# Sliding-window attention with a gated conv FFN: attention output turned by DMA for batches 2 to 7, and a re-planned lead-in

## The chip, the cores and the metric

One core of a Trainium2 chip runs the whole program. In the views PE is the tensor engine (its weight loads are PEld), DVE is VectorE, ACT is ScalarE, POOL is GpSimd, and SPq is the sync queue, which issues DMA transfers. PEclk is the granted clock of PE, as a share of full speed. The metric is device time in microseconds (us). Most of the numbers below come from the profile of one execution ("span") or from a few timed runs.

## The reference, cut to what matters

```python
# q, k, v: [8 batches, 8 heads, 576 positions, 64]
scores = where(|i - j| <= 32, q @ k.T / 8, -1e9)
x = softmax(scores) @ v          # -> [8, 576, 512] (heads side by side)
h = relu(x @ w_in)               # 512 -> 1024
conv = sum_k conv_w[k] * shift(h, k - 1)      # 3 taps along the sequence
out = (h * sigmoid(conv)) @ w_out             # 1024 -> 512, float32
```

The first FFN product contracts over the 512 features, so each batch's attention output (positions on the partitions, features along the row) has to be turned: features onto partitions. That turn is the subject.

## The kernel before

The work is cut into jobs. Each job has a planned time and a list of jobs that must precede it, and jobs are given out in the order of the planned times. Planned times set an order, and which jobs of the lead-in (the stage before the first output) are held in program order; nothing else. Inside one kernel a scheduler still moves instructions unless they are marked `fixed`. The FFN runs in chunks of 384 positions, three for each pair of batches: `ph` (first product), `pc` (conv and gate), `py` (second product and a store).

The turn (`job_xt`): four 128x128 matmuls against the identity, then one PSUM copy on VectorE.

```python
def job_xt(b, c):                       # batch b, block c of 5
    ...
    ps = slot_f().rearrange("p (k x) -> p k x", k=KC)
    for kc in range(KC):
        nc.tensor.matmul(ps[:, kc, 0:cols], xn[b][:, c, 2 * kc:2 * kc + 2, :]..., ident[:, 0:cols], ...)
    (vector.tensor_copy if b > 1 or c % 2 else nc.scalar.copy)(
        out=xT[b // 2][:, :, b % 2, 128 * c:128 * c + cols], in_=ps[:, :, 0:cols])
```

The value tile is needed twice, once shifted by 64 partitions (`vo`). For batch 1 VectorE copies it, for later batches a DMA from the ScalarE queue:

```python
def shift_v(b):
    for p0, src in ((0, ve[64:128, 0:NBLK - 1]), (64, ve[0:64, 1:NBLK])):
        if b == 1:
            vector.tensor_copy(out=vo[p0:p0 + 64], in_=src)
        else:
            fixed(nc.scalar.dma_start(vo[p0:p0 + 64], src))
```

Planned times that matter here (`P` = 29 us per batch, `NP` = 4 head pairs per batch):

```python
T0, T1 = 22.0, 42.5                     # start of chunk 0, second half of chunk 1
...                                     # start[c]: later chunks
end = start[3 * (b // 2) + 1] - 3.0 - (0 if b % 2 else 20.0 if b == 2 else P)
d = P / NP if b > 3 else 5.0            # spacing of the four head pairs of batch b
s0 = max(end - 5.9 * d, pair[b * NP - 1][0] + d)      # first head pair
...
at(("xt", b, c), t + (2.0 + 0.06 * c) * d ...)        # turns, after the last head pair at t
```

Weights are loaded as float32 and cast to bf16 on GpSimd, half a weight (128x2048) to an instruction. During the lead-in only VectorE is held in program order (`vector.on`).

The softmax here doesn't subtract the row's maximum and nothing guards it: scores larger than these inputs give would overflow.

Of the kernel before, what the change touches and what calls it, by code (L numbers as in the profile page):

```python
# [17 lines left out]
def kernel(  # L18
# [58 lines left out]
    class InOrder:  # L77


        on = False  # L80

        def __getattr__(self, name):
            def give(*args, **kwargs):
                ins = getattr(nc.vector, name)(*args, **kwargs)  # L84
                return fixed(ins) if self.on else ins

            return give

    vector = InOrder()

# [41 lines left out]
    def shift_v(b):  # L132

        ve, vo = ve_pp[b % NLD], vo_pp[b % NLD]
        for p0, src in ((0, ve[64:128, 0:NBLK - 1]), (64, ve[0:64, 1:NBLK])):
            if b == 1:
                vector.tensor_copy(out=vo[p0:p0 + 64], in_=src)
            else:
                fixed(nc.scalar.dma_start(vo[p0:p0 + 64], src))

# [42 lines left out]
    def load_weight(src, dst, rows, cast_):  # L183

        n = src.shape[1] // 2
        for x in (0, n):
            st = {}

            def load(x=x, st=st):
                t_ = fpool.tile([128, rows * n], FP32, name="wst", tag="wst")  # L190
                st[0] = t_.rearrange("p (c f) -> p c f", c=rows)
                fixed(nc.sync.dma_start(
                    st[0], src.rearrange("(c p) f -> p c f", p=128)[:, :, x:x + n]
                ))

            yield load, lambda x=x, st=st: cast_(dst[:, :, x:x + n], st[0])

# [10 lines left out]
    def job_tr(g2, y):  # L208

        b, i = g2 // NPH, g2 % NPH  # L210
        nat = qkb_pp[b % NLD][y][i]
        to = []
        for g in (2 * g2, 2 * g2 + 1):
            if y == 0:
                t_ = apool.tile([128, S], BF16, name="qT", tag="qT", bufs=4)
                to.append(t_)
            else:
                t_ = kT_pp[g % NKT]
                to.append(t_[:, PAD:PAD + S])
            state["qk"[y], g] = t_  # L220

        small = b == 0
        for js in ((range(0, 4), range(4, 8), range(8, RP)) if small else (range(RP),)):
            j0, n = js[0], len(js)
            ps = slot_f() if small else slot_a()
            for j in js:
                nc.tensor.matmul(  # L227
                    ps[:, 128 * (j - j0):128 * (j - j0) + 128],
                    nat[:, j, :, :].rearrange("p e d -> p (e d)"),
                    ident, start=True, stop=True,  # L230
                )
            rows = ps[:, 0:128 * n].rearrange("p (j y x) -> p y x j", j=n, y=2)
            for x, copy in enumerate((nc.scalar.copy, vector.tensor_copy)):
                copy(
                    out=to[x].rearrange("p (x j) -> p x j", j=RP)[:, :, j0:j0 + n], in_=rows[:, x]
                )

    def job_conv_w():
        ps = slot_f()
        nc.tensor.matmul(ps[:, 0:3 * MB], conv_w24, ident24, start=True, stop=True)  # L240
        vector.tensor_copy(out=conv_w_sb.rearrange("p k m -> p (k m)"), in_=ps[:, 0:3 * MB])
# [8 lines left out]
    def job_sc(g):  # L250
        qT, kT = state.pop(("q", g)), state.pop(("k", g))
        ps, last = slot_a(), slot_f()
        for i in range(NT):
            for e, t in ((0, (i + NT - 1) % NT), (1, i)):
                nc.tensor.matmul(  # L255
                    last[:, 0:64] if e * t == NT - 1 else ps[:, col(e, t):col(e, t) + 64],
                    kT[64 * e:64 * e + 64, 64 * t:64 * t + 128],
                    qT[64 * e:64 * e + 64, 64 * t:64 * t + 64],
                    start=True, stop=True,
                )  # L260
        attn = apool.tile([128, 2 * S], BF16, name="attn", tag="attn", bufs=4)
        state["a", g] = attn
        x = 2 * S - 64
        nc.scalar.activation(attn[:, 0:x], ps[:, 0:x], AF.Exp, bias=0.0, scale=scale)  # L264
        nc.scalar.activation(attn[:, x:], last[:, 0:64], AF.Exp, bias=0.0, scale=scale)  # L265
        vector.tensor_tensor(out=attn, in0=attn, in1=mask, op=ALU.mult)

    def job_av(g):
# [7 lines left out]
        for e in range(2):  # L276
            for c in range(NBLK):
                for j in range(2):
                    t = min(2 * c + j, NT - 1)
                    nc.tensor.matmul(  # L280
                        pss[e][64 * j:64 * j + 64, 65 * c:65 * c + 65],
# [10 lines left out]
        for e, (po, rec, to) in enumerate(outs):  # L292
            if b == 0 and e == 1 and pr < 3:
                for c in range(NBLK):
                    nc.scalar.activation(
                        to[:, c, :], po[:, c, 0:64], AF.Copy, bias=0.0, scale=rec[:, c:c + 1]
                    )
# [6 lines left out]
    def job_xt(b, c):  # L304

        if b % 2 == 0 and c == 0:
            xT[b // 2] = fpool.tile([128, KC, 2, S], BF16, name="xT", tag="xT")
        cols = min(128, S - 128 * c)
        ps = slot_f().rearrange("p (k x) -> p k x", k=KC)
        for kc in range(KC):  # L310
            nc.tensor.matmul(  # L311
                ps[:, kc, 0:cols],
                xn[b][:, c, 2 * kc:2 * kc + 2, :].rearrange("p h d -> p (h d)"),
                ident[:, 0:cols], start=True, stop=True,
            )
        (vector.tensor_copy if b > 1 or c % 2 else nc.scalar.copy)(
            out=xT[b // 2][:, :, b % 2, 128 * c:128 * c + cols], in_=ps[:, :, 0:cols]
# [13 lines left out]
    def job_ph(c, m, halves=(0, 1)):  # L331
# [8 lines left out]
        for kc in range(KC):  # L340
            nc.tensor.matmul(  # L341
                ps[:, 0:n], w_in_sb[:, kc, m * 128:(m + 1) * 128], x_[:, kc, x0:x1],
                start=(kc == 0), stop=(kc == KC - 1),
            )
        if kind == 1:
            out_ = hT[:, m, :].rearrange("p (i x) -> p i x", i=2)
            for i in halves:
                o_ = out_[:, i, i:i + HW + 1]
                i_ = ps[:, (HW + 1) * (i - halves[0]):(HW + 1) * (i - halves[0]) + HW + 1]
                if halves == (0, 1):  # L350
                    continue
                nc.scalar.activation(o_, i_, AF.Relu, bias=0.0, scale=0.5)
            if halves == (0, 1):
                base = hT[:, m, 0:HW + 1]
                both = bass.AP(base.tensor, base.offset, [list(base.ap[0]), [HW + 3, 2], [1, HW + 1]])
                nc.scalar.activation(
                    both, ps[:, 0:n].rearrange("p (i x) -> p i x", i=2), AF.Relu, bias=0.0, scale=0.5
                )
        else:
            o0 = 1 if kind == 0 else 0  # L360
            nc.scalar.activation(hT[:, m, o0:o0 + n], ps[:, 0:n], AF.Relu, bias=0.0, scale=0.5)  # L361

    def job_pc(c, m, halves=(0, 1)):
# [14 lines left out]
        for kk in range(3):  # L378
            nc.tensor.matmul(  # L379
                ps[:, 0:n], diag_w[:, kk, m, :], taps(kk), start=(kk == 0), stop=(kk == 2)  # L380
            )
        tn = spool.tile([128, CH], FP32, name="tn", tag="tn")
        nc.scalar.activation(tn[:, 0:n], ps[:, 0:n], AF.Tanh, bias=0.0, scale=1.0)  # L383
        vector.scalar_tensor_tensor(
# [8 lines left out]
    def job_py(c, i):  # L393

        ps = slot_f()
        for m in range(MB):
            nc.tensor.matmul(  # L397
                ps, gT[c][:, m, 128 * i:128 * i + 128], w_out_sb[:, m, :],
                start=(m == 0), stop=(m == MB - 1),
            )  # L400
        y_sb = spool.tile([128, d_model], FP32, name="y_sb", tag="y_sb", bufs=4)
        nc.scalar.copy(out=y_sb, in_=ps)  # L402
        r0 = c * CH + 128 * i
# [16 lines left out]
    def give_out():  # L420
# [9 lines left out]
        while ready:  # L430
            _, _, key = heapq.heappop(ready)
            vector.on = plan[key][0] < T0 + 14.0
            plan[key][1]()
# [7 lines left out]

    T0, T1 = 22.0, 42.5
    start = {0: T0, 1: T1}
# [21 lines left out]
    for m in range(MB):  # L465
        at(("diag", m), T0 + 1.6 * m - 1.0, lambda m=m: make_diag(m), ("conv_w",))
    at(("conv_w",), 7.0, job_conv_w)
# [15 lines left out]
    for b in range(B):  # L483
# [4 lines left out]
        else:  # L488
            end = start[3 * (b // 2) + 1] - 3.0 - (0 if b % 2 else 20.0 if b == 2 else P)
            d = P / NP if b > 3 else 5.0  # L490
            s0 = max(end - 5.9 * d, pair[b * NP - 1][0] + d)
        for i in range(NP):
            pair[b * NP + i] = (s0 + i * d, d)
    for g in range(NG):
# [4 lines left out]
        if b == 0:  # L499
            t0, t1, t2, t3 = 5.8 + 1.35 * (g // 2) * 2, 7.2 + 1.35 * (g // 2) * 2, 8.4 + 2.0 * g, 16.2 + g  # L500
        else:
# [9 lines left out]
    for b in range(B):  # L511
        t, d = pair[b * NP + NP - 1]
        for c in range(NBLK):
            at(("xt", b, c), t + (2.0 + 0.06 * c) * d if b else 20.3 + 0.4 * c, lambda b=b, c=c: job_xt(b, c),
               *[("av", b * NP + i) for i in range(NP)],
               *[("ph", (b // 2 - 2) * 3 + 2, m, None) for m in range(MB)])
        t0 = pair[b * NP][0]
        for i, (ld, cs) in enumerate(load_stream(b)):
            if b == 0:
                x, y = -20.0, 20 + (4.3 + 1.35 * i if i < NP else 9.8 + 1.1 * (i - NP))  # L520
            elif b == 1:
# [3 lines left out]
            else:  # L525
                x, y = t0 - P - 3.0 + i * P / NV, 4.5
            at(("load", b, i), x, ld if b else lambda: None, ("load", b, i - 1),
               *[("cast", b - 1, j) for j in range(NV)],
# [8 lines left out]
    for i, (ld, cs) in enumerate(load_weight(moe_w_in, w_in_sb, KC, cast)):  # L537
        at(("w_in load", i), -1.0, ld, *[("load", 0, j) for j in range(NV)])
        at(("w_in", i), 16.5 + 2.0 * i, cs, ("w_in load", i))
    for i, (ld, cs) in enumerate(load_weight(moe_w_out, w_out_sb, MB, cast)):  # L540
# [33 lines left out]
```

## Time and profile before

| | us |
|---|---|
| time, median of 4 runs (of 3: 286.14) | 285.45 (284.67 to 286.53) |
| profiled span | 282.2 |
| PE busy | 246.8 (87%) |
| VectorE / ScalarE / GpSimd busy | 181.5 / 175.9 / 77.1 |

I cut each span at three events: the ScalarE copy of the first output rows of chunk 0, of the last rows of chunk 3, and of the first rows of chunk 9. That gives four stages: lead-in, first rounds (chunks 0 to 3 come out), later rounds (chunks 4 to 8), tail. This is the busy-time table of the kernel before for these stages. Its columns are the stretch, its length, the busy time of each engine with the number of instructions, the mean granted PE clock, the DMA share and GB/s.

```profile
core 0: us, PE busy (x) PEld busy (x) DVE busy (x) ACT busy (x) POOL busy (x), PEclk, DMA share, GB/s
0.00:71.34 71.34, 47.62 (x586) 33.88 (x588) 55.34 (x135) 39.37 (x93) 40.56 (x44) 0.90 0.87 251
71.34:143.53 72.19, 69.12 (x839) 42.85 (x847) 50.02 (x106) 49.70 (x105) 19.48 (x22) 1.00 0.62 170
143.53:249.22 105.69, 100.95 (x1079) 60.29 (x1094) 68.34 (x140) 68.73 (x139) 17.01 (x18) 1.00 0.43 123
249.22:282.20 32.98, 29.11 (x155) 15.19 (x156) 7.82 (x14) 18.14 (x36) 0.00 (x0) 0.99 0.20 72
```

In the lead-in PE is idle for 24 us and the mean clock is 0.90. The same table for those instructions alone that write or read the attention output `xn` shows what the turns cost PE in the two middle stages:

```profile
core 0: us, PE busy (x) PEld busy (x) DVE busy (x) ACT busy (x), PEclk, DMA share, GB/s
71.34:143.53 72.19, 3.18 (x40) 2.47 (x40) 10.13 (x22) 0.00 (x0) 1.00 0.62 170
143.53:249.22 105.69, 5.34 (x80) 4.91 (x80) 11.74 (x26) 0.00 (x0) 1.00 0.43 123
```

The PE columns are turns alone: 80 matmuls take 5.34 us of the later rounds, so a batch of 20 costs 1.33 us. The copies that follow them are in the view of the turned tile (duration in ns as minimum/median/maximum):

```profile
L84 DVE CAST xT<-pf x34: 406/680/693, 27.4 to 245.8; 128x512 bf16<-128x512 f32 x28, 128x256 bf16<-128x256 f32 x6
```

What PE waited for in the later rounds (total us, times, longest):

```profile
PE pf L379 <- DVE rec L84: 1.5, 2, 0.7
PE pa L227 <- DVE qT L84: 1.1, 2, 0.5
PE pf L341 <- DVE xT L84: 0.6, 1, 0.6
PE pf L255 <- DVE xT L84: 0.4, 1, 0.4
```

These named waits come to 3.6 us, all on VectorE, and only 1.0 us of that is on the copies of the turns (`xT`).

The bad place of the lead-in, in four-microsecond stretches:

```profile
36.00:40.00 4.00, 3.28 (x49) 1.73 (x47) 3.36 (x10) 3.46 (x8) 0.38 (x1) 1.00 1.08 358
40.00:44.00 4.00, 1.50 (x30) 1.21 (x29) 3.94 (x4) 1.47 (x2) 3.17 (x2) 0.80 1.06 390
44.00:48.00 4.00, 3.59 (x11) 1.30 (x10) 4.00 (x7) 1.46 (x4) 3.40 (x4) 0.50 1.17 273
48.00:52.00 4.00, 3.32 (x34) 2.31 (x35) 3.54 (x9) 1.06 (x3) 1.81 (x2) 0.50 0.40 89
```

VectorE is full from 40 to 48 us and PE waits. Then PE runs at half its clock until 52 us: it does 11 matmuls in a stretch in which it counts as 3.59 us busy. In that stretch a first-product matmul takes up to 0.53 us; the median of these over the span is 0.33 us. The Trainium skill ("TensorE: Matmul & The Clock Gate", Part 1) describes this: a clock gate at 4/8 after an idle window, 8/8 after sustained work.

### The profile page before, as it was taken

What the parts mean: (1) busy time and instruction counts of PE and PEld (TensorE: products, weight loads), DVE (VectorE), ACT (ScalarE), POOL (GpSimd) and SP (SyncE); (2) the same over time, 40 slices, a digit from 0 to 9 for tenths busy, and PEclk for the clock granted to TensorE, in tenths of its full rate; (3) what the DMA queues carried; (4) which work ended last, traced back from release to release, by engine and by line L of the source; (5) the groups of instructions that cost most, each with busy time, mean ns of one, the idle gap of its engine ahead of it and who ended that gap; (6) DMA issues with size and microseconds to landing.
All of it is one profiled execution on the core that took longest, in us unless ns stands there. A gap on an engine that the chain in (4) does not pass through costs nothing.

```text
span 282.2 us, 6681 instructions
## 1 busy us (share of the span) xinstructions
PE 246.8 (87%) x2652; PEld 152.2 (54%) x2682; DVE 181.5 (64%) x394; ACT 175.9 (62%) x370; POOL 77.1 (27%) x84
## 2 busy tenths in 40 slices
PE   1756767877999898999989999999989999999994
PEld 1535433656665554666555555565555655555551
DVE  5687989795465888486556767596656555733330
ACT  2755672565676666677765577766755677557652
POOL 5657738661026221043113412332200000000000
PEclk9999995797999999999999999999999999999999
DMA  6999999781687742784649564954240102011022
GB/s 231 253 329 360 210 365 256 193 280 32 171 207 239 199 114 66 231 272 118 148 95 310 156 161 131 306 165 114 65 115 37 39 37 78 37 39 74 37 78 112
DMA packets 55555, 45.58 MB, mean 162 GB/s; under 512 B 38860, under 2 KB 40932, under 8 KB 55524
## 3 DMA queue, kind: packets, MB, share of 16 engines
q1 hardware_dynamic: 54528, 41.95, 50.7%
q10 hardware_dynamic: 996, 3.21, 4.9%
q8 instruction: 21, 0.34, 0.6%
q14 instruction: 10, 0.08, 0.1%
HBM read 32.52 MB, written 9.44 MB: 149 GB/s over the span
## 4 chain that ended last, share of the span: by engine, by line
PE 70%; DVE 19%; ACT 5%; DMA 3%; issue 2%; SPq 1%; POOL 0%; DVEq 0%; ACTq 0%
PE pf L397 21%; PE pf L341 20%; PE pf L379 14%; PE pa L227 5%; PE pf L280 4%; DVE attn L84 3%; DVE xT L84 3%; DVE gT L84 3%; DMA kst<-in_k_dram 3%; DVE vo L84 3%; PE pa L255 3%; DVE diag_w L84 2%; ACT attn L264 2%; PE pf L311 2%; DVE xn L84 2%
## 5 line engine op out<-in xcount | busy, mean ns | idle before, releaser
L84 DVE SCALAR_TENSOR_TENSOR gT<-tn,hT 128x384 bf16<-128x384 f32 (+1 forms) x104 | 60.2, 587 | 43.2 <-ACT tn L383 42.9
L341 PE MATMUL pf<-xT,w_in_sb 128*128 128x385 bf16 (+2 forms) x416 | 81.3, 322 | 3.7 <-DVE xT L84 2.2
L379 PE MATMUL pf<-hT,diag_w 128*128 128x384 bf16 (+1 forms) x312 | 66.0, 320 | 2.6 <-DVE rec L84 1.5
L397 PE MATMUL pf<-w_out_sb,gT 128*128 128x512 bf16 x258 | 66.4, 380 | 1.6 <-issue 0.2
L383 ACT ACTIVATE tn<-pf 128x384 f32<-128x384 f32 (+1 forms) x104 | 49.0, 472 | 12.4 <-PE pf L379 11.8
L341 PEld LDWEIGHTS <-w_in_sb 128*128 128x128 bf16 x416 | 38.8, 100 | 27.1 <-DVE xT L84 2.0
L109 POOL TENSOR_SCALAR ve<-vst 128x512 bf16<-128x512 f32 x40 | 28.6, 719 | 60.8 <-DMA vst<-in_v_dram 37.7
L402 ACT COPY y_sb<-pf 128x512 f32<-128x512 f32 x36 | 21.1, 586 | 38.2 <-PE pf L397 35.8
L397 PEld LDWEIGHTS <-gT 128*128 128x128 bf16 x288 | 27.7, 98 | 29.3 <-issue 0.3
L361 ACT ACTIVATE hT<-pf 128x385 bf16<-128x385 f32 x64 | 31.8, 497 | 14.0 <-PE pf L341 13.4
L379 PEld LDWEIGHTS <-diag_w 128*128 128x128 bf16 x312 | 28.2, 99 | 20.9 <-issue 1.8
L264 ACT ACTIVATE attn<-pa 128x1088 bf16<-128x1088 f32 x32 | 34.5, 1079 | 7.2 <-PE pf L255 3.8
L84 DVE TENSOR_TENSOR attn<-attn,mask 128x1152 bf16<-128x1152 bf16 x32 | 27.1, 846 | 7.8 <-ACT attn L265 5.8
L109 POOL TENSOR_SCALAR qb<-qst 128x1152 bf16<-128x1152 f32 x16 | 19.3, 1204 | 35.6 <-DMA qst<-in_q_dram 32.5
L84 DVE TENSOR_TENSOR xn<-pf,rec 128x320 bf16<-128x320 f32 x61 | 27.8, 482 | 0.8 <-DVE rec L84 0.2
L84 DVE CAST xT<-pf 128x512 bf16<-128x512 f32 (+1 forms) x34 | 20.4, 634 | 9.6 <-PE pf L311 9.6
L109 POOL TENSOR_SCALAR kb<-kst 128x1152 bf16<-128x1152 f32 x16 | 19.1, 1194 | 19.1 <-DMA kst<-in_k_dram 12.2
L280 PEld LDWEIGHTS <-attn 128*64 128x64 bf16 x640 | 14.7, 119 | 16.5 <-issue 8.8
L280 PE MATMUL pf<-ve,attn 128*64 128x65 bf16 x384 | 19.2, 207 | 5.0 <-DVE attn L84 3.6
L255 PEld LDWEIGHTS <-kT 64*128 64x128 bf16 x576 | 12.7, 98 | 13.5 <-issue 6.7
L280 PE MATMUL pf<-vo,attn 128*64 128x65 bf16 x256 | 17.2, 207 | 3.0 <-DVE vo L84 3.0
L84 DVE RECIPROCAL rec<-pf 128x5 f32<-128x5 f32 x64 | 10.4, 181 | 14.1 <-PE pf L280 13.6
(54 smaller groups left out, 206.4 us busy)
## 6 DMA issues: line engine op xcount, KB each, us to landing
qst<-in_q_dram SPq DMA_DIRECT2D x16, 576.0 KB, 6.4
kst<-in_k_dram SPq DMA_DIRECT2D x16, 576.0 KB, 7.6
out_dram<-y_sb SPq DMA_DIRECT2D x36, 256.0 KB, 2.2
vst<-in_v_dram SPq DMA_DIRECT2D x24, 256.0 KB, 4.6
vo<-ve ACTq DMA_DIRECT2D x12, 260.0 KB, 5.3
vst<-in_v_dram SPq DMA_DIRECT2D x16, 192.0 KB, 4.6
wst<-in_moe_w_in_dram SPq DMA_DIRECT2D x2, 1024.0 KB, 8.3
wst<-in_moe_w_out_dram SPq DMA_DIRECT2D x2, 1024.0 KB, 9.5
```

What stands on the lines that cost most here:

```text
L84: ins = getattr(nc.vector, name)(*args, **kwargs)
L109: fixed(nc.gpsimd.tensor_scalar(out=out_, in0=in_, scalar1=1.0, scalar2=0.0, op0=ALU.mult, op1=ALU.add))
L227: nc.tensor.matmul(ps[:, 128 * (j - j0):128 * (j - j0) + 128], nat[:, j, :, :].rearrange("p e d -> p (e d)"), ident, start=True, stop=True,)
L255: nc.tensor.matmul(last[:, 0:64] if e * t == NT - 1 else ps[:, col(e, t):col(e, t) + 64], kT[64 * e:64 * e + 64, 64 * t:64 * t + 128], qT[ ...
L264: nc.scalar.activation(attn[:, 0:x], ps[:, 0:x], AF.Exp, bias=0.0, scale=scale)
L280: nc.tensor.matmul(pss[e][64 * j:64 * j + 64, 65 * c:65 * c + 65], attn[:, col(e, t):col(e, t) + 64], (ve if t % 2 == 0 else vo)[:, t // 2 ...
L341: nc.tensor.matmul(ps[:, 0:n], w_in_sb[:, kc, m * 128:(m + 1) * 128], x_[:, kc, x0:x1], start=(kc == 0), stop=(kc == KC - 1),)
L361: nc.scalar.activation(hT[:, m, o0:o0 + n], ps[:, 0:n], AF.Relu, bias=0.0, scale=0.5)
L379: nc.tensor.matmul(ps[:, 0:n], diag_w[:, kk, m, :], taps(kk), start=(kk == 0), stop=(kk == 2))
L383: nc.scalar.activation(tn[:, 0:n], ps[:, 0:n], AF.Tanh, bias=0.0, scale=1.0)
L397: nc.tensor.matmul(ps, gT[c][:, m, 128 * i:128 * i + 128], w_out_sb[:, m, :], start=(m == 0), stop=(m == MB - 1),)
L402: nc.scalar.copy(out=y_sb, in_=ps)
```

## The change

Its intent: give PE and VectorE less to do by letting DMA transposes on the sync queue do the turns of batches 2 to 7; plan attention earlier so that the slower turns are hidden; move the value shifts from VectorE (batch 1) and the ScalarE queue (later) to the sync queue; and re-plan the lead-in, with PE and ScalarE in program order too, some weight scaling (`diag`) earlier and weight casts in pieces.

```diff
-    vector = InOrder()
+    vector, scalar, tensor = InOrder(nc.vector), InOrder(nc.scalar), InOrder(nc.tensor)
@@ shift_v
-            if b == 1:
-                vector.tensor_copy(out=vo[p0:p0 + 64], in_=src)
-            else:
-                fixed(nc.scalar.dma_start(vo[p0:p0 + 64], src))
+            fixed(nc.sync.dma_start(vo[p0:p0 + 64], src))
@@ load_weight
-            yield load, lambda x=x, st=st: cast_(dst[:, :, x:x + n], st[0])
+            def casts(x=x, st=st):
+                step = 512 // n
+                for c in range(0, rows, step):
+                    cast_(dst[:, c:c + step, x:x + n], st[0][:, c:c + step])
+            yield load, casts
@@ job_xt
+        if b > 1:
+            fixed(nc.sync.dma_start_transpose(
+                out=xT[b // 2][:, :, b % 2, 128 * c:128 * c + cols],
+                in_=xn[b][0:cols, c, :, :].rearrange("p h d -> p (h d)"),
+            ))
+            return
@@ planned times
-    T0, T1 = 22.0, 42.5
+    T0, T1 = 23.0, 43.0
-        at(("diag", m), T0 + 1.6 * m - 1.0, ...)
+        at(("diag", m), (8.8, 9.0, 11.7)[m] if m < 3 else T0 + 1.6 * m - 1.5, ...)
-            d = P / NP if b > 3 else 5.0
-            s0 = max(end - 5.9 * d, pair[b * NP - 1][0] + d)
+            d = 6.6 if b > 3 else 5.0
+            s0 = max(end - 6.3 * d, pair[b * NP - 1][0] + d)
...   (jobs of batch 0 and casts of the first weight re-planned; loads of batches 2 and later issued after the value shift of batch 1; matmuls and ScalarE calls go through `tensor` and `scalar`)
```

More of the change, by code (lines that the diff above doesn't have):

```diff
@@ L80, with __init__ @@
         on = False
+        def __init__(self, engine):
+            self.engine = engine
         def __getattr__(self, name):
-            def give(*args, **kwargs):
-                ins = getattr(nc.vector, name)(*args, **kwargs)
-                return fixed(ins) if self.on else ins
-            return give
-    vector = InOrder()
+            do = getattr(self.engine, name)
+            return (lambda *args, **kwargs: fixed(do(*args, **kwargs))) if InOrder.on else do
+    vector, scalar, tensor = InOrder(nc.vector), InOrder(nc.scalar), InOrder(nc.tensor)
     def load_v(b, c):
@@ L226, in job_tr @@
             for j in js:
-                nc.tensor.matmul(
+                tensor.matmul(
                     ps[:, 128 * (j - j0):128 * (j - j0) + 128],
@@ L232, in job_tr @@
             rows = ps[:, 0:128 * n].rearrange("p (j y x) -> p y x j", j=n, y=2)
-            for x, copy in enumerate((nc.scalar.copy, vector.tensor_copy)):
+            for x, copy in enumerate((scalar.copy, vector.tensor_copy)):
                 copy(
@@ L239, in job_conv_w @@
         ps = slot_f()
-        nc.tensor.matmul(ps[:, 0:3 * MB], conv_w24, ident24, start=True, stop=True)
+        tensor.matmul(ps[:, 0:3 * MB], conv_w24, ident24, start=True, stop=True)
         vector.tensor_copy(out=conv_w_sb.rearrange("p k m -> p (k m)"), in_=ps[:, 0:3 * MB])
@@ L254, in job_sc @@
             for e, t in ((0, (i + NT - 1) % NT), (1, i)):
-                nc.tensor.matmul(
+                tensor.matmul(
                     last[:, 0:64] if e * t == NT - 1 else ps[:, col(e, t):col(e, t) + 64],
@@ L263, in job_sc @@
         x = 2 * S - 64
-        nc.scalar.activation(attn[:, 0:x], ps[:, 0:x], AF.Exp, bias=0.0, scale=scale)
-        nc.scalar.activation(attn[:, x:], last[:, 0:64], AF.Exp, bias=0.0, scale=scale)
+        scalar.activation(attn[:, 0:x], ps[:, 0:x], AF.Exp, bias=0.0, scale=scale)
+        scalar.activation(attn[:, x:], last[:, 0:64], AF.Exp, bias=0.0, scale=scale)
         vector.tensor_tensor(out=attn, in0=attn, in1=mask, op=ALU.mult)
@@ L279, in job_av @@
                     t = min(2 * c + j, NT - 1)
-                    nc.tensor.matmul(
+                    tensor.matmul(
                         pss[e][64 * j:64 * j + 64, 65 * c:65 * c + 65],
@@ L294, in job_av @@
                 for c in range(NBLK):
-                    nc.scalar.activation(
+                    scalar.activation(
                         to[:, c, :], po[:, c, 0:64], AF.Copy, bias=0.0, scale=rec[:, c:c + 1]
@@ L308, in job_xt @@
         cols = min(128, S - 128 * c)
+        if b > 1:
[4 more added lines that the diff above has]
+            return
         ps = slot_f().rearrange("p (k x) -> p k x", k=KC)
         for kc in range(KC):
-            nc.tensor.matmul(
+            tensor.matmul(
                 ps[:, kc, 0:cols],
@@ L315, in job_xt @@
             )
-        (vector.tensor_copy if b > 1 or c % 2 else nc.scalar.copy)(
+        (vector.tensor_copy if c % 2 else scalar.copy)(
             out=xT[b // 2][:, :, b % 2, 128 * c:128 * c + cols], in_=ps[:, :, 0:cols]
@@ L340, in job_ph @@
         for kc in range(KC):
-            nc.tensor.matmul(
+            tensor.matmul(
                 ps[:, 0:n], w_in_sb[:, kc, m * 128:(m + 1) * 128], x_[:, kc, x0:x1],
@@ L351, in job_ph @@
                     continue
-                nc.scalar.activation(o_, i_, AF.Relu, bias=0.0, scale=0.5)
+                scalar.activation(o_, i_, AF.Relu, bias=0.0, scale=0.5)
             if halves == (0, 1):
@@ L355, in job_ph @@
                 both = bass.AP(base.tensor, base.offset, [list(base.ap[0]), [HW + 3, 2], [1, HW + 1]])
-                nc.scalar.activation(
+                scalar.activation(
                     both, ps[:, 0:n].rearrange("p (i x) -> p i x", i=2), AF.Relu, bias=0.0, scale=0.5
@@ L360, in job_ph @@
             o0 = 1 if kind == 0 else 0
-            nc.scalar.activation(hT[:, m, o0:o0 + n], ps[:, 0:n], AF.Relu, bias=0.0, scale=0.5)
+            scalar.activation(hT[:, m, o0:o0 + n], ps[:, 0:n], AF.Relu, bias=0.0, scale=0.5)
     def job_pc(c, m, halves=(0, 1)):
@@ L378, in job_pc @@
         for kk in range(3):
-            nc.tensor.matmul(
+            tensor.matmul(
                 ps[:, 0:n], diag_w[:, kk, m, :], taps(kk), start=(kk == 0), stop=(kk == 2)
@@ L382, in job_pc @@
         tn = spool.tile([128, CH], FP32, name="tn", tag="tn")
-        nc.scalar.activation(tn[:, 0:n], ps[:, 0:n], AF.Tanh, bias=0.0, scale=1.0)
+        scalar.activation(tn[:, 0:n], ps[:, 0:n], AF.Tanh, bias=0.0, scale=1.0)
         vector.scalar_tensor_tensor(
@@ L396, in job_py @@
         for m in range(MB):
-            nc.tensor.matmul(
+            tensor.matmul(
                 ps, gT[c][:, m, 128 * i:128 * i + 128], w_out_sb[:, m, :],
@@ L401, in job_py @@
         y_sb = spool.tile([128, d_model], FP32, name="y_sb", tag="y_sb", bufs=4)
-        nc.scalar.copy(out=y_sb, in_=ps)
+        scalar.copy(out=y_sb, in_=ps)
         r0 = c * CH + 128 * i
@@ L431, in give_out @@
             _, _, key = heapq.heappop(ready)
-            vector.on = plan[key][0] < T0 + 14.0
+            InOrder.on = plan[key][0] < T0 + 14.0
             plan[key][1]()
@@ L465 @@
     for m in range(MB):
-        at(("diag", m), T0 + 1.6 * m - 1.0, lambda m=m: make_diag(m), ("conv_w",))
+        at(("diag", m), (8.8, 9.0, 11.7)[m] if m < 3 else T0 + 1.6 * m - 1.5, lambda m=m: make_diag(m), ("conv_w",))
     at(("conv_w",), 7.0, job_conv_w)
@@ L499 @@
         if b == 0:
-            t0, t1, t2, t3 = 5.8 + 1.35 * (g // 2) * 2, 7.2 + 1.35 * (g // 2) * 2, 8.4 + 2.0 * g, 16.2 + g
+            t0, t1 = ((6.0, 7.5), (10.5, 12.2))[g // 2]
+            t2, t3 = (9.4, 10.4, 14.7, 16.2)[g], 18.0 + 0.8 * g
         else:
@@ L513 @@
         for c in range(NBLK):
-            at(("xt", b, c), t + (2.0 + 0.06 * c) * d if b else 20.3 + 0.4 * c, lambda b=b, c=c: job_xt(b, c),
+            at(("xt", b, c), t + (2.0 + 0.06 * c) * d if b else 21.5 + 0.3 * c, lambda b=b, c=c: job_xt(b, c),
                *[("av", b * NP + i) for i in range(NP)],
@@ L519 @@
             if b == 0:
-                x, y = -20.0, 20 + (4.3 + 1.35 * i if i < NP else 9.8 + 1.1 * (i - NP))
+                x, y = -20.0, 20 + ((4.9, 6.4, 8.8, 10.9)[i] if i < NP else 12.1 + 1.25 * (i - NP))
             elif b == 1:
@@ L526 @@
                 x, y = t0 - P - 3.0 + i * P / NV, 4.5
-            at(("load", b, i), x, ld if b else lambda: None, ("load", b, i - 1),
+            at(("load", b, i), x, ld if b else lambda: None, ("load", b, i - 1), *[("vo", 1)][:b - 1],
                *[("cast", b - 1, j) for j in range(NV)],
@@ L538 @@
         at(("w_in load", i), -1.0, ld, *[("load", 0, j) for j in range(NV)])
-        at(("w_in", i), 16.5 + 2.0 * i, cs, ("w_in load", i))
+        at(("w_in", i), 17.2 + 1.0 * i, cs, ("w_in load", i))
     for i, (ld, cs) in enumerate(load_weight(moe_w_out, w_out_sb, MB, cast)):
```

## The prediction

> **What bounds the kernel now.** In the table of busy times the tensor engine (PE) is busy 246.8 of 282.2 us, 87%; VectorE has 181.5, ScalarE 175.9. The chain of waits is 70% PE, 19% VectorE. The busy-time table by stretches separates three stages. From 66 to 246 us the program repeats in rounds of two batches, 60.1 us each; PE is busy 57.1, 57.6 and 57.8 us of a round (95 to 96%): PE-bound. The last 36 us are PE work too. The lead-in (0 to 66 us) is different: PE is idle over 20 us, VectorE is busy 9.9 us of 40 to 50, the DMA engines are full (share about 1.0) from 10 to 46 us, and after PE idled at 40 to 43 us its granted clock is 0.5 until about 52 us.
>
> **Removed.** 30 turns (6 batches x 5 blocks): 120 weight loads with 120 matmuls against the identity. One round has 40, with 2.67 us of PE busy time, so 8.0 us in all, nearly all in PE-bound rounds. Also 30 PSUM copies on VectorE (630 ns mean, about 19 us, mostly off the path) and 12 DMA issues on ScalarE (536 ns median, 6 us of its queue).
>
> **Added.** 30 DMA transposes on the sync queue. No trace shows one yet. The Trainium skill ("DVE: VectorE Perf Modes", the three transpose paths) gives 1309 ns for 128x128 bf16. Four such tiles make a block and five blocks a batch: my estimate is 5 to 15 us per batch, at worst about 26 if tiles run singly. A batch has about 30 us, DMA share in rounds is 0.25 to 0.65, and the schedule moves attention earlier, leaving roughly 10 us between last attention output and use. Probably hidden. The queue is in order, so a transpose waiting for attention holds later loads and stores; loads lead by about 25 us and stores have four buffers, so this should not reach PE.
>
> **Lead-in.** Two VectorE copies (3.0 us) become DMA. Weight casts on GpSimd are cut from 2.2 to about 0.6 us pieces: three weight-scaling instructions that took 4.1 us at 43 us, beside such a cast, should take 0.6 to 1 us. Nine of these move ahead of 16 us. I expect 5 us less VectorE work after 30 us. But the shifted values now come by DMA behind 2 MB of weight loads in a full queue (the second half lands at 42.6 us before); the first attention output of batch 1 waits for that, at about 43 us as before, so PE may stall and lose clock again. Net gain 3 us, between -2 and 8.
>
> **Sum.** 286.1 - 7.5 (turns, less some waits) - 3 = 275.6. Predicted 275.5 us, with 268.5 to 283.5 holding 8 times in 10. Chances: faster by over 2% 0.77, within 2% 0.17, slower 0.06.
>
> **What would show it.** Rounds of 57 to 58 us instead of 60.1, PE busy 95% or more in them; PE total down about 8 us; VectorE down 19 us or more; PE waiting for the transposed tile under 1 us per batch; transposes landing within 10 us; the third chunk's first projections at about 63 us instead of 66.
>
> **What would make it wrong.** Transposes that take over 10 us per batch from output to landing: PE would wait in each round and the gain vanishes or reverses. In the lead-in a fixed PE order that waits too early (shifted values landing after 45 us), or, to the good, a clock that never drops, worth up to 5 us more.

(The page that this text cites bears the title "VectorE: DVE Perf Modes".)

## More of the kernel before

In the later rounds PE is busy 100.95 of 105.69 us. PE is the limit there, and it is idle for 4.7 us.

## The result, and the profile after

The changed kernel took 274.37 us in the median of 4 runs (273.39 to 278.23; the last one is slow), against 285.45 us. Executions over 1.5% slower than the fastest of the same kernel are left out of the means. The ratio is 0.9598, 95% interval 0.9536 to 0.9659: 4.0% faster. A ratio here is the mean time of one kernel's fast runs over that of the other's of the same rounds, so it is not quite the ratio of the medians. The predicted 275.5 us and its range hold. A second set of the changed kernel, run later as a control, gave 275.76 us (273.87 to 280.82) and 0.9712 (0.9642 to 0.9783). The ten runs together have the median 274.6 us; the eight of them that are not slow have 274.1 us.

The stages of the changed kernel:

```profile
core 0: us, PE busy (x) PEld busy (x) DVE busy (x) ACT busy (x) POOL busy (x), PEclk, DMA share, GB/s
0.00:69.33 69.33, 44.03 (x583) 31.55 (x585) 48.99 (x132) 38.01 (x91) 44.16 (x56) 0.95 0.98 267
69.33:143.48 74.15, 68.87 (x812) 41.86 (x820) 47.17 (x98) 50.58 (x107) 19.93 (x23) 0.98 0.77 192
143.48:238.70 95.22, 94.38 (x993) 54.92 (x1005) 56.50 (x118) 68.56 (x137) 16.88 (x18) 1.00 0.66 152
238.70:271.70 33.00, 29.11 (x155) 15.19 (x156) 7.82 (x14) 18.14 (x36) 0.00 (x0) 0.98 0.19 72
```

Of the 10.5 us between the two spans, the lead-in gives 2.0, the first rounds *lose* 2.0, the later rounds give 10.5 and the tail nothing. That is not how I had spread it. In the later rounds PE has 6.6 us less to do (100.95 to 94.38) and its idle time falls from 4.7 to 0.8 us.

What PE waited for in the whole span (the longest rows):

```profile
PE pf L87 <- POOL qb L109: 6.7, 2, 6.0
PE pf L87 <- DMA vo<-ve: 3.8, 1, 3.8
PE pf L349 <- DMA xT<-xn: 3.7, 2, 2.6
PE pf L87 <- DVE vo L87: 3.4, 2, 1.8
```

The first row is the start of the program, when nothing has been loaded yet, and was there before (6.2 us). The second and third are new. The third is PE waiting for turned tiles: two times, at 103.1 and 124.9 us, both in the first rounds (batches 2 and 3), none later. The wait is followed by a slow clock, as these stretches show (PE busy 2.90 of 2.90 us at a clock of 0.50):

```profile
100.00:103.10 3.10, 0.52 (x4) 0.13 (x2) 1.23 (x2) 1.10 (x3) 0.50 (x1) 0.98 0.73 148
103.10:106.00 2.90, 2.90 (x25) 1.70 (x25) 0.69 (x2) 0.49 (x1) 0.36 (x2) 0.50 0.71 199
```

The second row of the waits has its reason in the chain of waits between 30 and 48 us (start, duration, what):

```profile
34.27 0.63 POOL ve L109
...
34.92 9.19 DMA vo<-ve
44.11 0.04 issue
44.15 0.48 PE pf L87 x19
```

The shifted values of batch 1 are ready to go at 34.9 us and land 9.2 us later. In the sync queue they were issued behind 2 MB of output weights. PE stands still, and its clock drops:

```profile
40.00:44.00 4.00, 0.22 (x1) 0.21 (x2) 1.86 (x5) 0.19 (x1) 3.16 (x6) 1.00 1.03 241
44.00:48.00 4.00, 3.76 (x52) 2.47 (x52) 2.87 (x7) 2.21 (x4) 2.13 (x3) 0.62 1.05 391
```

The transposes themselves (the view of their line, durations are the time that one holds the sync queue):

```profile
L312 SPq DMA_TRANSPOSE xT<-xn x30: 1195/1257/2779, 94.5 to 230.6; - x30
...
DMA to landing us min/median/max: 2.3/3.1/6.2
```

Each holds the queue for 1.26 us in the median, and the five of a batch take 6.5 to 9.8 us from the first issue to the end of the last, with other transfers between them in most batches. The PE turns of a batch cost 1.33 us of PE time.

The queue itself makes the two waits longer. The last attention output of batch 2 is written until 92.5 us. The transposes then stand behind the store of an output tile, which is not computed before 94.0 us:

```profile
92.06 0.48 DVE L301 TENSOR_TENSOR xn<-pf,rec 128x320 bf16<-128x320 f32 x1
94.06 0.37 SPq L412 DMA_DIRECT2D out_dram<-y_sb  x1
94.53 4.56 SPq L312 DMA_TRANSPOSE xT<-xn  x3
```

So the first transpose of batch 2 is issued 2.0 us after its data are there, and that of batch 3, behind another store, 1.5 us. My estimate from these numbers: without the stores ahead of them, some 3 of the 3.7 us of waits would not be there. No run tests it.

### The profile page after: what moved, and what is told of

Same layout as the page of the kernel before. It is cut to its first block, busy times and chain, and to the rows that moved or that the text cites. A ratio compares the mean times of both kernels' runs of the same rounds, so it can differ in the third digit from the quotient of the medians.

```text
span 271.7 us, 6447 instructions
## 1 busy us (share of the span) xinstructions
PE 236.4 (87%) x2535; PEld 143.5 (53%) x2562; DVE 160.5 (59%) x362; ACT 175.3 (65%) x370; POOL 81.0 (30%) x96
## 3 DMA queue, kind: packets, MB, share of 16 engines
q1 hardware_dynamic: 70432, 49.22, 70.6%
## 4 chain that ended last, share of the span: by engine, by line
PE 68%; DMA 15%; DVE 5%; SPq 4%; ACT 3%; issue 2%; POOL 0%
PE pf L405 22%; PE pf L349 20%; PE pf L387 14%; DMA kst<-in_k_dram 5%; PE pa L229 4%; DMA vst<-in_v_dram 4%; PE pf L282 4%; DMA vo<-ve 3%; PE pa L257 3%; DMA xT<-xn 3%; SPq L95 2%; DVE attn L268 1%; SPq L312 1%; DVE gT L392 1%; DVE diag_w L87 1%
## 5 line engine op out<-in xcount | busy, mean ns | idle before, releaser
L392 DVE SCALAR_TENSOR_TENSOR gT<-tn,hT 128x384 bf16<-128x384 f32 (+1 forms) x96 | 55.7, 585 | 55.7 <-ACT tn L391 55.6
L349 PE MATMUL pf<-xT,w_in_sb 128*128 128x385 bf16 (+2 forms) x380 | 73.6, 317 | 4.9 <-DMA xT<-xn 3.7
L387 PE MATMUL pf<-hT,diag_w 128*128 128x384 bf16 (+1 forms) x288 | 59.0, 314 | 0.7 <-ACT hT L360 0.6
L349 PEld LDWEIGHTS <-w_in_sb 128*128 128x128 bf16 x380 | 34.4, 98 | 25.9 <-issue 3.3
L369 ACT ACTIVATE hT<-pf 128x385 bf16<-128x385 f32 x56 | 27.7, 496 | 10.8 <-PE pf L349 10.1
L266 ACT ACTIVATE attn<-pa 128x1088 bf16<-128x1088 f32 x26 | 27.9, 1074 | 4.7 <-PE pf L257 3.9
L268 DVE TENSOR_TENSOR attn<-attn,mask 128x1152 bf16<-128x1152 bf16 x26 | 20.9, 804 | 10.4 <-ACT attn L267 9.6
L364 ACT ACTIVATE hT<-pf 128x386 bf16<-128x386 f32 x24 | 11.9, 494 | 4.4 <-PE pf L349 4.0
L282 PE MATMUL pf<-ve,attn 128*64 128x65 bf16 x312 | 13.8, 199 | 0.3 <-DVE attn L268 0.3
L257 PE MATMUL pa<-qT,kT 64*128 64x64 bf16 x442 | 12.3, 191 | 0.9 <-DVE kT L236 0.9
L282 PE MATMUL pf<-vo,attn 128*64 128x65 bf16 x208 | 12.9, 200 | 0.0
```

Source lines behind the costliest of these rows:

```text
L257: tensor.matmul(last[:, 0:64] if e * t == NT - 1 else ps[:, col(e, t):col(e, t) + 64], kT[64 * e:64 * e + 64, 64 * t:64 * t + 128], qT[64 ...
L266: scalar.activation(attn[:, 0:x], ps[:, 0:x], AF.Exp, bias=0.0, scale=scale)
L268: vector.tensor_tensor(out=attn, in0=attn, in1=mask, op=ALU.mult)
L282: tensor.matmul(pss[e][64 * j:64 * j + 64, 65 * c:65 * c + 65], attn[:, col(e, t):col(e, t) + 64], (ve if t % 2 == 0 else vo)[:, t // 2, h ...
L349: tensor.matmul(ps[:, 0:n], w_in_sb[:, kc, m * 128:(m + 1) * 128], x_[:, kc, x0:x1], start=(kc == 0), stop=(kc == KC - 1),)
L369: scalar.activation(hT[:, m, o0:o0 + n], ps[:, 0:n], AF.Relu, bias=0.0, scale=0.5)
```

## The experiments

The change has three parts that can be had separately: **the lead-in** (everything before about 40 us, and the value shifts on the sync queue), **the attention times** (the two numbers 6.6 and 6.3), and **the DMA turns**. My theory A, from the prediction: the turns are the gain (8 us of PE work), the lead-in adds 2 to 3 us. Rival B: attention times and the freed ScalarE queue bring it.

### 1. The DMA turns alone

```diff
 # on the kernel before
+        if b > 1:
+            fixed(nc.sync.dma_start_transpose(out=xT..., in_=xn...)); return
```

> The kernel before with the DMA turns of batches 2 to 7 alone; schedule, lead-in and value shifts as before. Theory A (the gain is the turns: 8 us of PE work and the waits that their VectorE copies caused): 276.5 to 279 us, that is 6.5 to 9 us under the kernel before, rounds after the first near 56 us; a PE wait of 3 to 8 us for the first DMA-turned batches, whose attention ends late. Rival B (the gain comes from the retimed attention, and DMA turns at the old times reach PE too late): within 2 us of before, with PE waiting for the turned tile in every round.

Measured: 287.86 us (285.89 to 288.55, 4 runs), ratio 1.0115 (1.0055 to 1.0175). The turns alone make the kernel *slower*. Theory A falls here. PE lost what it had gained to two waits in the later rounds; this is the timeline of PE where it first needs batch 5:

```profile
186.46 2.72 PE L347 MATMUL pf<-xT,w_in_sb 128*128 128x386 bf16 x8 [2.35 <-DMA xT<-xn]
```

The busy-time table just after it (clock 0.51), and the sync queue ahead of it, with the last attention output of batch 5:

```profile
187.00:190.00 3.00, 3.00 (x29) 1.51 (x28) 0.28 (x2) 0.98 (x2) 0.00 (x0) 0.51 0.37 67
```

```profile
179.23 0.87 DVE L84 TENSOR_TENSOR xn<-pf,rec 128x320 bf16<-128x320 f32 x2
182.06 0.36 SPq L410 DMA_DIRECT2D out_dram<-y_sb  x1
182.51 6.46 SPq L310 DMA_TRANSPOSE xT<-xn  x5
```

The five transposes are issued from 182.5 to 189.0 us, and PE wanted the tile at 184.1. The bracket gives the idle time before the group and who ended it. Batch 7 is the same at 246.7 us, with 4.4 us. The plan explains part of it. By the planned times, from the last attention output of batches 5 and 7 to the first FFN chunk that needs it there are 5.1 us in the kernel before. That was enough for PE turns. (This chunk needs the first two blocks of batch 5; PE starts once the second has landed, at 186.3 us.) The rest is the queue: the outputs of batch 5 were complete at 180.1 us, but the transposes stood behind an output store until 182.5 us, 2.4 us that are as long as the PE wait; for batch 7 it was 2.5 of 4.4 us. So turns behind stores need more room than turns alone. A run with the transposes ahead of these stores, which could show how much the old times matter then, was not made.

### 2. Everything but the DMA turns

```diff
 # on the changed kernel
-        if b > 1:
+        if False:
...
-        (vector.tensor_copy if c % 2 else scalar.copy)(
+        (vector.tensor_copy if b > 1 or c % 2 else scalar.copy)(
```

> The changed kernel with the turns of batches 2 to 7 back on PE and VectorE: lead-in, value shifts on the sync queue and attention times as changed. Theory A: 282.5 to 285 us, 1 to 3 us under before (only the lead-in's 2 us remain). Rival B (retimed attention and the ScalarE queue freed of DMA issues bring the gain): 276 to 279 us.

Measured: 276.54 us (275.89 to 278.22, 4 runs), ratio 0.972 (0.9666 to 0.9775). Most of the gain is there without the named part of the change. That is what rival B had expected. PE's later rounds:

```profile
143.03:243.28 100.25, 99.78 (x1086) 59.38 (x1085) 66.91 (x138) 68.84 (x138) 16.14 (x18) 1.00 0.42 120
```

PE still does all its turns and has 0.5 us of idle time left in 100 us (4.7 in 106 before). The idle time of the kernel before went away without touching the turns.

### 3. The changed kernel with the old attention times

```diff
-            d = 6.6 if b > 3 else 5.0
-            s0 = max(end - 6.3 * d, ...)
+            d = P / NP if b > 3 else 5.0
+            s0 = max(end - 5.9 * d, ...)
```

> The changed kernel with the two numbers of the attention times put back (batches 4 and on spaced as before, start 5.9 instead of 6.3 spacings ahead). Theory A: within 1.5 us of the changed kernel, PE waits for the turned tile under 1 us in the later rounds. Rival B: 3 us or more slower than the changed kernel, with PE waits for the turned tile in the later rounds.

Measured: 282.2 us (279.71 to 283.61, 4 runs), ratio 0.9918 (0.9842 to 0.9993): by the medians 6 to 8 us slower than the changed kernel (against its second and its first set), with 5.4 us of PE waits for turned tiles, both in the later rounds. Rival B's number again. With the new times the planned room for batches 5 and 7 is 10.8 and 14.2 us instead of 4.6. With the queue as it is, two constants decide whether the DMA turns pay.

### 4. DMA turns kept, PE turns done for nothing

```diff
             fixed(nc.sync.dma_start_transpose(...))
+            ps = slot_f()...
+            for kc in range(KC):
+                nc.tensor.matmul(ps[:, kc, 0:cols], xn[b]..., ident[:, 0:cols], start=True, stop=True)
             return
```

> The changed kernel, DMA turns kept, and the 120 PE turns issued besides into PSUM buffers that nobody reads (correct result). It costs the PE work of the turns alone, without the VectorE copies. If PE work is all of the gain of the later rounds: slower than the changed kernel by 8 us or more. Theory A (PE work 8 us, of which 6 to 7 on the path, and the copies' waits besides): slower by 5.5 to 7.5 us, PE waits in later rounds still under 1 us per round.

Measured: 277.83 us (277.66 to 278.18, 4 runs), ratio 0.9775 (0.9732 to 0.9818), 3.2 us over the changed kernel's pooled median (by the ratios 1.8 to 5.0 us over its two sets). That is under what either reading had expected (5.5 us or more). In the profiles the later rounds take 99.22 instead of 95.22 us and the first rounds 75.34 instead of 74.15. So PE work is on the path in the later rounds (4.0 us for 80 matmuls that count 5.3 us busy there before), and hardly in the first rounds, where PE waits anyway. With the copies besides (experiment 2) the later rounds take 100.25, so the 20 VectorE copies of that stage may be worth about 1 us; the two kernels differ in the DMA transposes too, and each length is from one profile.

### 5. The attention times alone, and 6. the lead-in alone

I now held theory C: three parts, and the DMA turns need the new times. Experiment 5 is the kernel before with the diff of experiment 3 the other way round; experiment 6 puts the edits of experiments 2 and 3 together.

> The kernel before with only the two numbers of the attention times changed; turns stay on PE. Theory C, formed after theory A fell (the gain has three parts: the lead-in, the attention times, which end the 4.7 us that PE idled between 143 and 249 us, and the DMA turns, which need those times): 279.5 to 282 us, PE waits after 140 us under 1 us. Rival (the times matter only to the DMA turns, and the lead-in brings the rest): 284 to 286 us.

> The changed kernel with PE turns and the old attention times: only the lead-in and the value shifts on the sync queue are changed. Theory C: 280.5 to 283 us, about 3 us under before; the later rounds keep their 4 to 5 us of PE idle time. Rival (lead-in brings the rest): 276 to 278 us.

Measured: times alone 283.14 us (6 runs), ratio 0.9963 (0.9916 to 1.001); lead-in alone 279.6 us (6 runs), ratio 0.9838 (0.9793 to 0.9882). The times alone are not clear of nothing, less than I expected. Their named PE waits after 140 us did fall to 1.3 us in total (from 3.6), and the later rounds shortened by 2.6 us, but in the profiled run, its slowest, the first rounds (1.2 us longer) and the lead-in (2.8) took back more. In that profile PE is idle for 2.6 of the later rounds' 103.1 us, 4.7 of 105.7 before. The lead-in alone gives 4.5 us, 1.5 times what I had predicted for it. That lies between the two expectations: below the 280.5 us of theory C, above the 278 of its rival. Its profile was its fastest run, and only 1.6 us of it is there at the first output rows; the first rounds gave 1.7 us, the later ones 2.4. There too PE is idle for 2.6 us in the later rounds, against the 4 to 5 us that I had expected to stay.

### 7. DMA turns and new times, without the new lead-in

> The kernel before with the DMA turns and the new attention times, without the new lead-in and with the value shifts on the ScalarE queue. It completes the table of three parts. Theory C (the DMA turns pay only with the new times; then about 1.2%): 278.5 to 281 us, 0.98 to 0.988 of before, PE waits for turned tiles only in the first round. If the turns need the new lead-in too: 283 us or more, with such waits later.

Measured: 283.6 us (279.83 to 286.45, 6 runs), ratio 0.9912 (0.9836 to 0.9987); three of the six are slow, and the other three have the median 280.5 us. The ratio is short of what I expected. The PE waits for turned tiles (4.9 us) were in the first rounds only, as expected.

The eight combinations now stand side by side. The stage lengths are read as in the two tables above, from one profile each; the time is the ratio to the kernel before.

| lead-in | times | DMA turns | kernel | ratio | lead-in us | first rounds | later rounds | tail |
|---|---|---|---|---|---|---|---|---|
| - | - | - | before | 1 | 71.3 | 72.2 | 105.7 | 33.0 |
| - | - | x | exp. 1 | 1.0115 | 72.3 | 70.8 | 110.8 | 33.0 |
| - | x | - | exp. 5 | 0.9963 | 74.1 | 73.4 | 103.1 | 32.9 |
| - | x | x | exp. 7 | 0.9912 | 70.9 | 76.8 | 98.1 | 33.0 |
| x | - | - | exp. 6 | 0.9838 | 69.8 | 70.5 | 103.3 | 33.0 |
| x | - | x | exp. 3 | 0.9918 | 70.3 | 68.5 | 110.1 | 33.0 |
| x | x | - | exp. 2 | 0.972 | 71.0 | 72.0 | 100.3 | 33.2 |
| x | x | x | changed | 0.9598, 0.9712 | 69.3 | 74.2 | 95.2 | 33.0 |

Read it by pairs of rows that differ in one mark. Later rounds: DMA turns gain 5.0 us with the new times, in both lead-ins (103.1 to 98.1, 100.3 to 95.2), and lose 5 to 7 us with the old ones. First rounds: the other way round. DMA turns gain 1.4 to 2.0 us with the old times and lose 2.1 to 3.4 with the new ones. All waits for turned tiles in the profiles agree with this: in the later rounds with old times, in the first rounds with new ones. The planned times of batches 2 and 3 are the same in both cases; what the new times change around them, so that their tiles come late, is settled in part only. For batch 2 the stores ahead of the transposes are not it: with either lead-in they hold the first transpose as long with the old times as with the new (2.0 us with the new lead-in, 3.6 without). But with the new times one load stands between the third and the fourth transpose (0.6 us; none with the old times), and the fourth lands 3.2 to 3.9 us after its issue instead of 2.5.

### 8. The turns of batches 2 and 3 back on PE

```diff
-        if b > 1:
+        if b > 3:
```

> The changed kernel with batches 2 and 3, whose DMA-turned tiles PE waits 3.7 us for, turned by PE again. Theory C (late tiles of the first round cost about what their PE work would): 272 to 275 us, no PE wait for turned tiles. If late tiles cost only their 3.7 us: 275 us or more, if the clock drop after them costs as much again: 271 us.

Measured: 272.47 us (270.13 to 274.85, 6 runs), ratio 0.9561 (0.9514 to 0.9608), about 2 us under the changed kernel's pooled 274.6. The intervals overlap with that of its first set, but each of the five fast runs (270.13 to 272.82) is under each of the changed kernel's eight (273.39 or more), which ran in other calls. The first rounds take 71.45 us instead of 74.15, with 0.7 us of PE waits for turned tiles left, later on. This profile is of the run marked slow, whose lead-in was 3.3 us longer. So the DMA turns of these two batches seem to cost some 2 us more than the 2.7 us of PE work that they saved.

### 9. The shifted values of batch 1 ahead of the output weights

```diff
-        at(("w_out load", i), 0.0, ld, *[("load", 1, j) ...], ("w_in", i))
+        at(("w_out load", i), 0.0, ld, *[("load", 1, j) ...], ("w_in", i), ("vo", 1))
```

> The changed kernel with the shifted values of batch 1 issued ahead of the 2 MB load of the output weights. If they land late because they queue behind that load (9.2 us in the changed kernel): they land within 5 us, the 3.8 us PE wait goes, and the time is 271 to 273 us unless the later weights hold up the first output rows. Rival (landing is slow by itself, or another wait takes its place): wait stays near 3 us, 273.5 to 275 us.

Measured: 269.49 us (269.21 to 271.85, 6 runs), ratio 0.9496 (0.9454 to 0.9538). This is the fastest kernel, 5 us under the changed one, and its runs scatter less. The wait on `vo` by DMA is gone from PE's list, and PE goes on with the attention output of batch 1 at 40.1 us, after a short wait for VectorE, instead of 44.15. The stretch where PE stood still:

```profile
40.00:44.00 4.00, 3.27 (x57) 2.20 (x58) 3.80 (x15) 3.18 (x8) 0.55 (x1) 1.00 0.99 322
44.00:48.00 4.00, 3.33 (x66) 2.71 (x66) 3.37 (x8) 2.61 (x6) 3.56 (x6) 1.00 1.06 380
```

The lead-in takes 64.56 us instead of 69.33: more than the 3.8 us of the wait; the clock stays at 1.00 there as well. The two shifts landed 3.4 and 3.7 us after their issue, within the 5 us that I had expected. Output weights that arrive later held up nothing that shows: the first output rows come earlier.

### 10. The value shifts of batches 2 to 7 back on the ScalarE queue

```diff
-            fixed(nc.sync.dma_start(vo[p0:p0 + 64], src))
+            fixed((nc.sync if b == 1 else nc.scalar).dma_start(vo[p0:p0 + 64], src))
```

> The changed kernel with the value shifts of batches 2 to 7 back on the ScalarE queue. The lead-in-only kernel gained 2 us at the first output rows but 5 us in the end; if the rest came from freeing ScalarE of 12 DMA issues (6 us of its queue): 2 to 3 us slower than the control. If ScalarE has the room: within 1 us of the control.

Measured: 277.22 us (275.22 to 279.24, 6 runs), ratio 0.9764 (0.9711 to 0.9817), against 0.9712 (0.9642 to 0.9783) of the control in the same rounds: 1.5 us by the medians of all runs, 3.0 by those of the fast ones, intervals overlapping. The profile, of its slowest run, has 97.3 us in the later rounds, 2.0 more than the control's 95.2. The direction fits the 2.4 us that the lead-in-only kernel won in its later rounds, but by time alone it is not clear of noise.

### 11. The control

> The changed kernel itself once more, as the control for the other three of this call: 272.5 to 275 us, 0.955 to 0.965 of before.

Measured: 275.76 us (273.87 to 280.82, 6 runs), ratio 0.9712. It missed the expected 0.955 to 0.965. Three runs are near 274 us, two near 277.4, one at 280.8. The profiled one waited 6.2 us for the shifted values where the first profile waited 3.8. This wait differs from run to run, and experiment 9 removes it; it may be a reason of the scatter. That is not shown: the slower runs have no profiles, and the profiled run with the 2.4 us longer wait took only 0.5 us more than the first one.

### 12. Experiment 9 with the attention of batch 3 planned 3 us earlier

```diff
-            end = start[3 * (b // 2) + 1] - 3.0 - ...
+            end = start[3 * (b // 2) + 1] - (6.0 if b == 3 else 3.0) - ...
```

> The kernel with the shifted values of batch 1 first, and besides the attention of batch 3 placed 3 us earlier, so that its DMA turns end before PE asks for them. If that wait (1.5 us in the profile, and the clock drop near it) is what is left in the first rounds: 267 to 269 us and no PE wait for turned tiles. If the earlier attention only crowds VectorE: 269.5 to 271 us.

Measured: 270.59 us (269.29 to 271.87, 6 runs), ratio 0.9543 (0.9496 to 0.9589): no gain over experiment 9. The first rounds shortened (73.8 us instead of 75.1) and the lead-in grew (66.9 instead of 64.6), and a wait for a turned tile of 1.7 us stayed. The edit did not get what it was for: from the last attention output of batch 3 to PE's first demand for its tile there are 6.4 us in both profiles, and 1.5 us of them the transposes stand behind an output store. That earlier attention crowds the lead-in fits its length, but was not taken apart. Not run: experiments 8 and 9 together.

## Why the prediction was right in its number, and where it was wrong inside

The time was right: 275.5 us predicted, 274.37 measured, and a direction with 0.77. The sum behind it was "286.1 - 7.5 (turns, less some waits) - 3". The experiments give another one. Adding the parts in the order lead-in, times, turns, the ratios go 0.984, 0.972, then 0.960 or 0.971: about 4.5, 3.4 and 0.2 to 3.5 us (a ratio step times 284 us). Two errors cancelled; that the number came out within 1.2 us was luck.

- **The mis-sized term: the turns, 7.5 us.** They gave at most 3.5 us with everything else in place, and cost about 3 us alone. The arithmetic of PE work was right: about 8 us busy, and in the later rounds the 5.0 us that four batches should give (4 x 1.33 = 5.3) arrived. But the step "Probably hidden" failed for the first rounds: PE waited 3.7 us for the tiles of batches 2 and 3 and then ran at half clock for a while, so those batches lost 2.1 us where 2.7 should have come. I read the "roughly 10 us between last attention output and use" as one number for all batches. By the plan it is 8.2 and 8.8 us for batches 3 and 2, and 10.8 and more later. In the trace the room is 6.4 and 8.0 us for these two, and from the last output to the last landing it took 11.2 and 10.9 us, more than the 10 us that the prediction had named as what would make it wrong. It had asked what a waiting transpose holds up, and not what a waiting store holds up: 1.5 and 2.0 us of this the transposes stood behind a store.
- **The missing term: the attention times.** I treated them as cover for the transposes. They also ended a part of the idle time that PE spent behind VectorE in the later rounds: 4.7 us before, 2.6 with the times alone, 2.6 with the lead-in alone, 0.5 with both. From experiment 6 to experiment 2 these rounds shortened by 3.0 us. Alone, without the new lead-in, the times gave 1.0 us, which is not clear of nothing. I subtracted "some waits" that the change would add, and never priced the waits already there. Why this earlier spacing keeps VectorE from holding PE up was not taken apart.
- **The lead-in, 3 us.** Alone it was 4.5 us, inside the range given. The part that I had named (VectorE relief) can't be split from the rest by these runs. The scaling instructions beside the cast did not come to "0.6 to 1 us": three still took 2.41 us, now beside another, uncut cast of GpSimd of 1.75 us. Part of the gain may be the ScalarE queue, which I had counted in us (6) and given no value; experiment 10 points that way and is not clear of noise.
- **What was predicted and seen.** PE waits for the shifted values at about 43 us "as before" and loses its clock: it waited until 44.15, with 0.62 after it, and experiment 9 shows that this was worth about 5 us. A transpose lands within 10 us of its issue (2.3 to 6.2) and a batch takes 5 to 15 us of queue (6.5 to 9.8). "Rounds of 57 to 58 us": from chunk 4's first product to chunk 7's and on to chunk 10's it took 56.3 and 52.5 us (60.3 and 58.4 before), but 60.6 us (59.2 before) from the second half of chunk 1 to chunk 4, where PE waited for turned tiles. VectorE's total fell by 21 us (19 or more predicted). PE's total fell by 10.4 us instead of 8; 3.6 us of that are in the lead-in, where no turn was moved and the mean clock rose from 0.90 to 0.95. The "third chunk" of the prediction was a misreading: the projections at 66 us belong to the second half of chunk 1 (64.4 us after); the third chunk starts at 78.8 us instead of 80.5, so the gain there is 1.7 us and not 3. "Under 1 us per batch" of PE waits for turned tiles held for batches 4 to 7 and failed for batches 2 and 3 (2.6 and 1.1 us).

## What to carry to other kernels

Moving work from the busy engine to a DMA here replaced 1.3 us of engine time by about 10 us from the last input to the last landing, for each batch. It pays only where the schedule has that room for *every* user of the result, so check the slack batch by batch before counting the saved work. A change that comes with re-planned times must be taken apart with the times as a factor of their own: here the same DMA turns lost 5 to 7 us or gained 5 us in the later rounds, by two constants. And an in-order queue is a schedule too: two shifts of 260 KB behind 2 MB of loads cost about 5 us, more than all the turns gained, and transposes stood up to 4.7 us behind transfers that were waiting for something else (batch 4 of experiment 1).

## What the Trainium skill lacked or had wrong

- "DMA: Bandwidth & Descriptors" (Issuing engines are not separate DMA queues) calls the sequencer's time to start a DMA "usually small relative to the DMA itself". No page gives a time to issue a transpose within SBUF under the name of trn2. Here a 128x512 bf16 transpose held the sync queue for 1.26 us, and landed 3.1 us after issue in the median. A plain 256 KB store held it for about 0.36 us.
- "VectorE: DVE Perf Modes" (The three transpose paths) has 1309 ns for a 128x128 bf16 DMA transpose and does not say between which events. Here one instruction of four such tiles held the queue for 1257 ns, so as queue time per tile the figure is four times too high for larger instructions; as time to landing it is too low, the median was 3.1 us.
- "DMA: Bandwidth & Descriptors" (Latency and other measured facts) gives 261 GB/s as effective rate of DMA transposes, 350 to 400 when contiguous. Here the sync queue's packets took 70.6% of 271.7 us in the changed kernel and 59.5% of 276.5 us in experiment 2, 27 us more for 3.54 MB more: about 130 GB/s, an estimate from these shares of one profile each, which hold other transfers too. The added packets average 239 bytes (14,784 packets).
- "TensorE: Matmul & The Clock Gate" (Part 1) has the clock fall after an idle window of about 3.4 us. Here waits of 2.58 us (changed kernel, at 100.5 us) and 2.32 us (experiment 9, at 51.1 us) were followed by a granted clock of 0.50 in the 3 us after the first and of 0.59 in the 4 us around the end of the second.
